# Two places for turned X, a new order of steps, and a shorter last dispatch in a banded attention with a soft mixture of experts

## The chip, the cores and the metric

The kernel runs on one core of one Trainium2 chip. The core has TensorE (PE, with its weight loads as PEld), VectorE (DVE), ScalarE (ACT), GpSimdE (POOL) and SyncE (SP, which issues most transfers), and 16 DMA engines. The metric is device time in microseconds (us); a kernel's time is the median of its runs. A profiled execution is one more run, with a record of each instruction.

## The reference

```python
def _attn_ref(q, k, v, n_global, n_local):          # B, H, S, D = 4, 8, 768, 64
    scores = scale * np.matmul(q, k.transpose(0, 1, 3, 2))
    rel = pos[:, None] - pos[None, :]
    is_global = pos[None, :] < int(n_global)         # 8
    is_local = (rel >= 0) & (rel < int(n_local))     # 96
    dist = np.where(is_global & ~is_local, float(n_local), np.abs(rel))
    scores = scores - slopes[:, None, None] * dist
    a = softmax(np.where(is_global | is_local, scores, -1e9))
    return np.matmul(a, v)

def _moe_ref(x, phi, w1, w2):                        # x: 3072 x 512, 8 experts, 4 slots each
    logits = x @ phi
    d = softmax(logits, over tokens); c = softmax(logits, over slots)
    slot_input = d.T @ x
    slot_out[e] = np.maximum(slot_input[e] @ w1[e], 0) @ w2[e]
    return c @ slot_out
```

Each query sees the first 8 keys and the 96 before it. The attention's output, 3072 tokens by 512, is the input X of the mixture: 32 slots are filled from all tokens, pass through two layers of weights (32 MB in all), and are spread over the tokens again.

## The kernel before

**Attention.** There are 16 units, u = 0 to 15: four batches by four pairs of heads. A unit is a row of steps. `load_qk` and `load_v` bring its inputs in, each into one of two places that alternate with u. `scores` (three steps, TensorE) multiplies queries and keys by bands of 120 into one of two pairs of PSUM banks (`sc`). `biased` (three steps, DVE) adds the table of the mask and the slope, and keeps the maximum. `max_t` and `max_r` (TensorE, DVE) make one shift of it. `exponential` (two heads, ACT) writes weights in float32, `w_hi` (ACT) casts them to float16, `w_lo` (three parts per head, POOL, or DVE as `w_lo_dve`) writes the rest that the cast left. `v_hi` and `v_lo` split v in the same way. `values` (per head, TensorE) multiplies 39 small products into the bank `x`. `ev_recs` and `ev_mul` (DVE) divide by the sums and write X. `tr` (two halves, TensorE) turns X and `tr_copy` (ACT, or DVE as `tr_copy_dve`) copies the turned half, 480 or 288 columns, into one of three places, the list `xtb`: a part of the tile `xta`, of `xtt` and of `tt`. `logits` (each second unit) multiplies the last two turned X with phi.

**Between batches** the steps `logits_half`, `logits_all`, `strip_exp`, `by_token`, `dispatch` and `dispatch_sum` carry the softmax over tokens on and add what the batch gives to the slots. For the last batch `last_dispatch` does this in one piece, with eight PSUM banks of which four are taken over from `sc` (the class `LeftBanks`, which hands banks out in a ring of six: the tags l0 to l3, and two of the pool `psm`).

**Mixture.** `hidden` (twice, four experts each) multiplies the slots with w1, `hidden_t` turns the result, `project` (twice two times) multiplies with w2 into 320 and then 192 output columns, `weights_by_slot` and `blocks_by_slot` bring the weights of the tokens into the tile `ct`, `combine` multiplies them with the slots' outputs and copies each product to an output buffer, which goes to memory.

**What sets the order.** `ORDER`, a list of steps written out in the file, holds the attention and the loads. It is walked once; each engine gets its instructions in that order and works them off one after the other. Transfers are issued by SP in the same order, and a transfer whose place is still being read holds up the ones behind it in SP's queue.

**Weights.** There are 32 pieces of 1 MB (128 x 2048). Ten have tiles of their own (`weights`). Others are loaded into tiles of the attention, when these come free: `piece` loads a whole one, `free(i)` loads into region i of the list `spaces`, `extra` loads the columns of a tile that the attention never uses. One piece lies in parts (`part`, the list `tails`): in a small tile `spare` and behind the ends of other tiles. A second piece has its first columns in `spare2` (`first`) and the rest where the first weight piece was, once that is used up.

**In the last dispatch** the function `warm_x` (L592 to L595) issues six matmuls whose product nobody reads. `warm` (L597 to L599) does the same at the start of the attention, 37 times.

Of the kernel before, what the change touches and what calls it, by code (L numbers as in the profile page):

```python
# [342 lines left out]
def tile_attention_moe(ctx: ExitStack, tc: tile.TileContext, qk, v, phi, w1, w2, nn, out):  # L343
# [34 lines left out]
    v16 = keep.tile([P, WP], F32, name="v16")  # L380
# [843 lines left out]
```

## Time and profile before

| | us |
|---|---|
| median of 3 runs | 195.08 |
| runs | 194.43 to 195.15 |
| the profiled execution | 194.77 |
| its span, first to last instruction | 193.0 |
| TensorE busy | 174.8 |
| DVE busy | 158.1 |
| ACT busy | 124.9 |
| POOL busy | 95.6 |

In the span the attention lasts to about 131 us, the last dispatch to 138, the two hidden layers and the first projection to 165, the second projection to 178. The last instruction that computes ends at 183, and the output's last transfers at about 190. 61.4 MB are moved in all. Rows of the profile name the source line, the engine, the operation and the tiles (out<-in); a row's first two numbers are start and length in us. Rows of the tables give a count and a mean. Names such as `m`, `sc`, `x`, `ld`, `cp` and `ctp` are PSUM banks; `tb` holds a unit's weights in float32, `ph` their two float16 parts.

### The profile page before, as it was taken

How to read it: one execution, taken by the hardware profiler on the slowest of the kernel's cores; microseconds unless marked ns; L12 is line 12 of the kernel's file. 1: busy time of each engine (PE TensorE's matmuls, PEld its weight loads, DVE VectorE, ACT ScalarE, POOL GpSimd, SP SyncE). 2: the span in 40 equal slices, each digit the busy share in tenths (PEclk: the TensorE clock that was granted, in tenths of full speed). 3: DMA queues.
4: the chain of work that ended last, by engine and by line, in shares of the span. 5: the costliest groups of instructions: out<-in, count | busy, mean ns of one | idle time of the engine just before them, and what ended most of it. 6: DMA issues, size and time to landing. Idle time of an engine off the chain costs nothing.

```text
span 193.0 us, 6494 instructions
## 1 busy us (share of the span) xinstructions
PE 174.8 (91%) x2676; PEld 130.3 (68%) x2676; DVE 158.1 (82%) x396; ACT 124.9 (65%) x162; POOL 95.6 (50%) x122
## 2 busy tenths in 40 slices
PE   8699999999999999998999999989999999799600
PEld 2355689788888879977878797875453366488500
DVE  3699799999998998999699999986797999772700
ACT  3107779998999998999899999924024161461500
POOL 7211936996688795797786897360001040000000
PEclk9999999999999999999999999999999999999965
DMA  2996756999499959999828679999999999479793
GB/s 71 401 394 195 269 186 202 358 396 364 162 404 346 410 186 364 423 410 378 310 87 317 270 256 360 409 420 420 400 401 416 421 418 419 164 257 356 259 324 123
DMA packets 19015, 61.40 MB, mean 318 GB/s; under 512 B 1824, under 2 KB 9632, under 8 KB 16416
## 3 DMA queue, kind: packets, MB, share of 16 engines
q1 hardware_dynamic: 17088, 59.55, 80.7%
q10 hardware_dynamic: 1888, 1.35, 2.1%
q8 instruction: 23, 0.38, 0.8%
q14 instruction: 16, 0.13, 0.2%
HBM read 54.59 MB, written 6.29 MB: 316 GB/s over the span
## 4 chain that ended last, share of the span: by engine, by line
PE 67%; DVE 10%; DMA 6%; ACT 6%; issue 3%; POOL 2%; ACTq 0%; DVEq 0%; POOLq 0%
PE sc L610 17%; PE x L670 14%; PE hp L127 8%; PE x L161 7%; DVE tb L619 4%; PE m L697 4%; DMA raw<-in_qk_dram 3%; PE cp L234 3%; DMA vt<-in_v_dram 3%; PE x L599 3%; PE m L798 2%; PE m L730 2%; POOL ph L645 2%; DVE v L588 2%; DVE xn L685 2%
## 5 line engine op out<-in xcount | busy, mean ns | idle before, releaser
L645 POOL TENSOR_TENSOR ph<-tb,ph 128x432 f16<-128x432 f32 x83 | 84.9, 1055 | 31.6 <-ACT ph L638 26.4
L635 ACT ACTIVATE tb<-tb,nb 128x1296 f32<-128x1296 f32 x32 | 43.1, 1373 | 9.9 <-DVE nb L631 9.9
L610 PE MATMUL sc<-raw 64*128 64x216 f32 (+2 forms) x448 | 45.7, 339 | 2.6 <-DMA raw<-in_qk_dram 1.6
L610 PEld LDWEIGHTS sc<-raw 64*128 64x128 f32 x448 | 37.0, 186 | 10.0 <-issue 4.0
L638 ACT CAST ph<-tb 128x1296 f16<-128x1296 f32 x31 | 39.4, 1269 | 4.9 <-PE x L670 4.3
L670 PE MATMUL x<-v,ph 128*128 128x65 f16 (+1 forms) x1209 | 41.7, 193 | 0.0
L670 PEld LDWEIGHTS <-ph 128*128 128x128 f16 x1248 | 39.8, 97 | 0.3
L588 DVE SCALAR_TENSOR_TENSOR v<-vt,v 128x896 f16<-128x896 f32 x16 | 18.7, 1171 | 0.5 <-ACT v L581 0.4
L619 DVE CUSTOM_DVE_ANT_1 tb<-sc,tt,mx 128x864 f32<-128x864 f32 x16 | 17.8, 1113 | 1.0 <-PE sc L610 0.3
L685 DVE CUSTOM_DVE_ANT_1 xn<-x,rcall 120x448 f32<-120x448 f32 x31 | 18.2, 619 | 0.4
L187 POOL TENSOR_TENSOR wp<-lnat,wp 120x512 f16<-120x512 f32 (+1 forms) x3 | 3.6, 1209 | 26.4 <-ACT wp L186 26.4
L581 ACT ACTIVATE v<-vt 128x896 f16<-128x896 f32 x14 | 13.3, 949 | 3.9 <-DMA vt<-in_v_dram 3.9
L697 PE MATMUL m<-ident,xn 120*128 120x120 f32 x105 | 15.4, 274 | 0.0
L197 DVE STREAM_TRANSPOSE wp<-wp 32x192 f32<-32x192 f32 (+1 forms) x32 | 12.9, 403 | 0.8
L697 PEld LDWEIGHTS m<-ident,xn 120*128 120x128 f32 x105 | 10.8, 141 | 1.6 <-issue 0.5
L127 PE MATMUL hp<-wp,sl 128*32 128x512 f32 x80 | 11.6, 595 | 0.0
L645 DVE TENSOR_TENSOR ph<-tb,ph 128x432 f16<-128x432 f32 x13 | 10.5, 815 | 0.1
L619 DVE CUSTOM_DVE_ANT_1 tb<-sc,xta,mx 128x864 f32<-128x864 f32 x8 | 8.9, 1108 | 1.3 <-PE sc L610 1.2
L619 DVE CUSTOM_DVE_ANT_1 tb<-sc,xtt,mx 128x864 f32<-128x864 f32 x8 | 8.9, 1113 | 0.4 <-PE sc L610 0.2
L619 DVE CUSTOM_DVE_ANT_1 tb<-sc,tt 128x864 f32<-128x864 f32 x8 | 8.4, 1054 | 0.9 <-POOL ph L645 0.4
L599 PE MATMUL x<-const-bfloat16-1.0 128*1 128x512 bf16 x37 | 9.2, 378 | 0.0
L234 PE MATMUL cp<-sots,ct 128*128 128x320 f32 (+1 forms) x48 | 8.4, 311 | 0.5 <-DVE sots L218 0.4
(224 smaller groups left out, 248.9 us busy)
## 6 DMA issues: line engine op xcount, KB each, us to landing
wp<-in_w_dram SPq DMA_DIRECT2D x15, 1024.0 KB, 8.9
raw<-in_qk_dram SPq DMA_DIRECT2D x15, 832.0 KB, 5.3
vt<-in_v_dram SPq DMA_DIRECT2D x16, 448.0 KB, 5.8
tb<-in_w_dram SPq DMA_DIRECT2D x3, 1024.0 KB, 7.4
raw<-in_w_dram SPq DMA_DIRECT2D x2, 1024.0 KB, 14.8
raw<-in_w_dram SPq DMA_DIRECT2D x2, 832.0 KB, 6.3
ph<-in_w_dram SPq DMA_DIRECT2D x2, 768.0 KB, 9.1
out_dram<-ph SPq DMA_DIRECT2D x2, 480.0 KB, 4.7
```

The costliest lines, as they stand in the source:

```text
L127: nc.tensor.matmul(out=hp[n][32 * s:32 * s + 32, :], lhsT=slv(a, c, s), rhs=w1(e, c // 2)[:, (c % 2) * DF + 512 * n:(c % 2) * DF + 512 * n ...
L234: nc.tensor.matmul(out=cp[:, w * i:w * i + w], lhsT=ct[:, t * P:t * P + P], rhs=sot, start=True, stop=True)
L588: nc.vector.scalar_tensor_tensor(out=vlo[k].rearrange("p j i d -> p (j i) d"), in0=vraw[k].rearrange("p j i d -> p (j i) d"), scalar=V_SC, ...
L599: nc.tensor.matmul(out=xx[0:1, 0], lhsT=busy_in[:, 0:1], rhs=busy_in, start=True, stop=True)
L610: nc.tensor.matmul(out=z[:, i, at:at + n], lhsT=r_[r, KCOL[j]:KCOL[j] + KR], rhs=r_[r, KW + KB * j:KW + KB * j + n], start=True, stop=True)
L619: nc.vector.tensor_tensor_reduce(out=tb(u)[:, :, BW * k:BW * k + BW], in0=sc[(3 * u + k) % 2][:, :, 0:BW], in1=table.unit(u % NP, k), scal ...
L635: nc.scalar.activation(out=t, in_=t, func=AF.Exp, bias=nbs[u], scale=T_SC)
L638: nc.scalar.copy(out=blocks(phi_[i])[:, :, 0:QW], in_=tb(u)[:, i].rearrange("p (s c) -> p s c", c=QW))
L645: (engine or nc.gpsimd).tensor_tensor(out=blocks(plo_[i])[:, c, 0:QW], in0=tb(u)[:, i].rearrange("p (s c) -> p s c", c=QW)[:, c], in1=bloc ...
L670: nc.tensor.matmul(out=x[:, (D + 1) * t:(D + 1) * t + d], lhsT=w[:, c:c + P], rhs=vv[:, j, i, 0:d], start=False, stop=(z == len(ops) - 1), ...
L685: nc.vector.tensor_tensor_reduce(out=xnb[(u // 2) % 3][:, :, c:c + D], in0=by_tile(x_bank(u, i))[0:KB, :, 0:D], in1=rcall[:, m, :].unsquee ...
L697: nc.tensor.transpose(out=m[:, at:at + KB], in_=xnb[(u // 2) % 3][:, t, P * (p % 2):P * (p % 2) + P], identity=ident[0:KB, 0:KB])
```

## The change

Five things are edited, and the list `ORDER` is another.

- `xtb` has two entries in place of three: the part of `tt` is gone, and `tt` shrinks from 2496 to 2048 columns. A turned X now goes to place u % 2. `spaces` has 17 regions in place of 18.
- `spare` holds 512 columns in place of 256 and `spare2` 448 in place of 256, so `part(0)` and `first` load more, and the piece in parts has four parts in place of five.
- For the last unit, `tr_copy` and `tr_copy_dve` halve each copy: the first half on ACT, the second on DVE.
- In `last_dispatch` the two calls of `warm_x` are gone, and each bank is named by its number in the ring (`at`).
- `by_slot(0)` stands ahead of the second half of the first projection and its copies are all on ACT; it stood behind that projection together with `by_slot(1)`.

```diff
-ORDER = [('load_v', 1), ('load_qk0', 0), ('load_phis', 0), ('load_qk', 0), ('load_v', 0),
+ORDER = [('load_v', 1), ('load_qk0', 0), ('load_phis', 0), ('load_qk', 0), ('load_v', 0),
...
-    tt = keep.tile([P, 2 * TABW + S], F32, name="tt")
+    tt = keep.tile([P, WP], F32, name="tt")
...
-    xtb = [xta[:, 0:S], xtt[:, 0:S], tt[:, 2 * TABW:2 * TABW + S]]
+    xtb = [xta[:, 0:S], xtt[:, 0:S]]
+    XTN = len(xtb)
...
-    spare = keep.tile([P, HF], F32, name="spare")
-    tails = [(0, HF, spare)] + [(HF * (2 * k + 1), HF * (2 * k + 3), tbt[i][:, WP:WP + 2 * HF]) for k, i in enumerate((1, 2, 0))]
-    tails.append((7 * HF, WP, tt[:, WP:WP + HF]))
+    spare = keep.tile([P, 2 * HF], F32, name="spare")
+    tails = [(0, 2 * HF, spare)] + [(2 * HF * k, 2 * HF * (k + 1), tbt[i][:, WP:WP + 2 * HF]) for k, i in ((1, 1), (2, 2), (3, 0))]
...
-    spare2 = keep.tile([P, 256], F32, name="spare2")
+    spare2 = keep.tile([P, 448], F32, name="spare2")
...
     def tr_copy(u, k):
         a, n = ((0, 4 * KB), (4 * KB, S - 4 * KB))[k]
-        nc.scalar.copy(out=xtb[u % 3][:, a:a + n], in_=ms.pop((u, k))[:, 0:n])
+        if u == last:
+            m = ms.pop((u, k))
+            nc.scalar.copy(out=xtb[u % XTN][:, a:a + n // 2], in_=m[:, 0:n // 2])
+            nc.vector.tensor_copy(out=xtb[u % XTN][:, a + n // 2:a + n], in_=m[:, n // 2:n])
+            return
+        nc.scalar.copy(out=xtb[u % XTN][:, a:a + n], in_=ms.pop((u, k))[:, 0:n])
...
-        mt = tile()
+        mt = tile(1)
         nc.tensor.transpose(out=mt[:, 0:P], in_=top.to_broadcast([P, P]), identity=ident)
-        warm()
-        warm()
...
-        mx = [tile(), tile()]
+        mx = [tile(2), tile(3)]
...
-        ml = tile()
+        ml = tile(4)
...
-        md, mz = [tile(), tile()], tile()
-        mg = tile()
+        md, mz = [tile(0), tile(1)], tile(2)
+        mg = tile(3)
...
     project(0, 0)
     moe.hidden_t(left, hss[1], hts[1])
+    for _, args in by_slot(0):
+        nc.scalar.copy(**args)
     moe.blocks_by_slot(spf[1], tps[1], (2, 0))
     nc.scalar.copy(out=ct[:, 3 * S:4 * S], in_=tps[1][:, 0:S])
     project(0, 1)
     slots_out(0)
-    copies = by_slot(0) + by_slot(1)
+    copies = by_slot(1)
     combine(0, 12, ((2, "DA", "S"),))
```

Counted over the list, POOL gets three `w_lo` more and DVE three fewer (nine leave DVE, six come to it); `v_hi` of unit 15 goes from ACT to DVE and `w_hi` of its first head from DVE to ACT; `v_hi` of unit 1 goes to POOL and those of units 0 and 7 to ACT. Six `tr_copy` change from ACT to DVE, and six others from DVE to ACT. SP has `load_qk` 1 to 4 and `load_v` 3 and 2 ahead of the first weight piece, and the `extra` loads, which were spread over the whole attention, now all come in its second half.

DVE at the start, behind the second `biased` of unit 0. L619 (now L613) is `biased`, its second row reads the maximum out; L339 writes the table of a pair of heads, L588 is `v_lo`, L631 (now L625) `max_r`. Before:

```order
L339 TENSOR_SCALAR tt<-tt 128x1728
L619 ISA tb_96,mx<-sc_177,tt,mx 128x2x432
L619 ISA mx 128x1
L619 ISA tb_97,mx<-sc_178,tt 128x2x432
L619 ISA mx 128x1
L631 ISA m,nb<-m,shift 128x128
L631 ISA nb 128x1
L339 TENSOR_SCALAR xta<-tt 128x1728
L588 SCALAR_TENSOR_TENSOR v_101<-vt,v_101 128x896
```

and with the change:

```order
L588 SCALAR_TENSOR_TENSOR v_101<-vt,v_101 128x896
L613 ISA tb_96,mx<-sc_177,tt,mx 128x2x432
L613 ISA mx 128x1
L339 TENSOR_SCALAR tt<-tt 128x1728
L625 ISA m,nb<-m,shift 128x128
L625 ISA nb 128x1
L588 SCALAR_TENSOR_TENSOR v_101<-vt,v_101 128x896
L613 ISA tb_97,mx<-sc_178,tt 128x2x432
L613 ISA mx 128x1
L339 TENSOR_SCALAR xtt<-tt 128x1728
```

Both `v_lo` come earlier, the first `max_r` stands ahead of the first `biased` of unit 1, and another table is written there.

TensorE in the last dispatch: `ld` are the banks of `LeftBanks`, `m` and `x` older banks, `dn` and `ex` the weights by token and by strip, `lsb` the logits. Before:

```order
L798 MATMUL m<-xn_106,dn 32x256 x7
L833 MATMUL ld<-ident,state 128x128
L595 LDWEIGHTS ident
L595 MATMUL x<-ident 128x256
...
L844 MATMUL ld<-ident,ex 120x128 x2
L775 MATMUL ld<-ident,lsb 120x128 x2
L798 MATMUL ld<-xn_107,dn 32x256 x7
```

and with the change:

```order
L799 MATMUL m<-xn_106,dn 32x256 x7
L834 MATMUL ld<-ident,state 128x128
L843 MATMUL ld<-ident,ex 120x128 x2
L776 MATMUL ld<-ident,lsb 120x128 x2
L799 MATMUL ld<-xn_107,dn 32x256 x7
```

The six matmuls of L595 are gone, and nothing else is moved.

ACT around the first combine: L148 copies the turned hidden layer, L994 (now L998) and L1004 (now L996 and L1005) write `ct`, L237 copies a product to an output buffer. Before:

```order
L148 COPY wp_92<-htp 128x512
L994 CAST ct<-wp_91 128x768
L237 COPY ph_99<-cp 128x320
L1004 CAST ct<-ctp 128x480 x2
L237 COPY ph_99<-cp 128x320
```

and with the change:

```order
L148 COPY wp_92<-htp 128x512
L996 CAST ct<-ctp 128x480
L996 CAST ct<-ctp 128x288
L998 CAST ct<-wp_91 128x768
L237 COPY tb_96<-cp 128x320
L1005 CAST ct<-ctp 128x480
L237 COPY tb_96<-cp 128x320
```

One of the two casts of 480 columns, and one of 288 that DVE had, now stand ahead of the projection's second half.

More of the change, by code (lines that the diff above doesn't have):

```diff
@@ L405, in tile_attention_moe @@
               ("ph0", (0, 2 * PH)), ("ph1", (0, 2 * PH)), ("v16", (0, VV)), ("v16", (VV, 2 * VV)),
-              ("vt", (0, VC)), ("vt", (VC, 2 * VC)), ("tt", (0, 2 * TABW)), ("tt", (2 * TABW, WP)), ("xta", (0, S)), ("xta", (S, S + TABW)),
+              ("vt", (0, VC)), ("vt", (VC, 2 * VC)), ("tt", (0, 2 * TABW)), ("xta", (0, S)), ("xta", (S, S + TABW)),
               ("xtt", (0, S)), ("xtt", (S, S + TABW)), ("xn", (0, XH))]
@@ L455, in first_of @@
     def first_of(k):
-        load_w([npl], 0, 256)
+        load_w([npl], 0, 448)
     def part_of(i):
@@ L565, in tile_attention_moe, with tile @@
         pool = None
-        def tile(self, shape, dtype, name, tag):
+        def tile(self, shape, dtype, name, tag, at=None):
             if self.pool is None:
@@ L570, in tile @@
                 self.pool = banks.enter_context(tc.tile_pool(name="psl", bufs=1, space=PSUM))
-            self.n += 1
+            self.n = self.n + 1 if at is None else at
             k = self.n % 6
@@ L589, in v_lo @@
                                        in1=vhi[k].rearrange("p j i d -> p (j i) d")[:, :, 0:D], op0=ALU.mult, op1=ALU.subtract)
-    idb = ident.bitcast(BF16)
-    def warm_x(u):
-        for n in (256, 256, P):
-            nc.tensor.matmul(out=xx[:, 0, 0:n], lhsT=idb[:, 0:P], rhs=idb[:, 0:n], start=True, stop=True)
     def warm(u, count):
@@ L701, in tr_copy @@
         a, n = ((0, 4 * KB), (4 * KB, S - 4 * KB))[k]
-        nc.scalar.copy(out=xtb[u % 3][:, a:a + n], in_=ms.pop((u, k))[:, 0:n])
+        if u == last:
[4 more added lines that the diff above has]
+        nc.scalar.copy(out=xtb[u % XTN][:, a:a + n], in_=ms.pop((u, k))[:, 0:n])
     def tr_copy_dve(u, k):
+        if u == last:
+            return tr_copy(u, k)
         a, n = ((0, 4 * KB), (4 * KB, S - 4 * KB))[k]
-        nc.vector.tensor_copy(out=xtb[u % 3][:, a:a + n], in_=ms.pop((u, k))[:, 0:n])
+        nc.vector.tensor_copy(out=xtb[u % XTN][:, a:a + n], in_=ms.pop((u, k))[:, 0:n])
     als, dns = {}, {}
@@ L729, in logits_of @@
             n = min(SW, S - SW * s)
-            nc.tensor.matmul(out=ms[u][32 * s:32 * s + 32, 0:n], lhsT=phis[:, units[u - k][1], :], rhs=xtb[(u - k) % 3][:, SW * s:SW * s + n],
+            nc.tensor.matmul(out=ms[u][32 * s:32 * s + 32, 0:n], lhsT=phis[:, units[u - k][1], :], rhs=xtb[(u - k) % XTN][:, SW * s:SW * s + n],
                              start=(k == 1), stop=(k == 0), skip_group_check=True)
@@ L817, in dispatch_sum, with last_dispatch, tile @@
             add_slots(b, m, slice(0, HF if b == B - 2 else DM))
-    def last_dispatch(left, warm):
+    def last_dispatch(left):
         b = B - 1
-        def tile():
-            return left.tile([P, 512], F32, name="ld", tag="x")
+        def tile(at):
+            return left.tile([P, 512], F32, name="ld", tag="x", at=at)
         mo = psm.tile([P, 512], F32, name="m", tag="m")
@@ L891, in table_pair @@
         table.pair(p)
-    steps = dict(piece=piece_of, free=free, part=part_of, first=first_of, extra=extra, load_qk0=load_qk0, load_phis=load_phis, keys=keys, warm_x=warm_x, warm=warm,
+    steps = dict(piece=piece_of, free=free, part=part_of, first=first_of, extra=extra, load_qk0=load_qk0, load_phis=load_phis, keys=keys, warm=warm,
                  table_a=table_a, table_b=table_b, table_pair=table_pair, load_qk=load_qk, load_v=load_v, v_hi=v_hi, v_hi_act=v_hi_act, v_hi_dve=v_hi_dve, v_lo=v_lo,
@@ L903, in tile_attention_moe @@
     left = LeftBanks()
-    rest = last_dispatch(left, lambda: warm_x(last))
+    rest = last_dispatch(left)
     fl = keep.tile([P, 12], F32, name="fl")
@@ L989, in combine, with by_slot @@
         moe.combine(left, ct, n, sots[:, at:at + w], obs, out, t0, plan)
+    def by_slot(b):
+        return moe.weights_by_slot(left, sps[b], ct, [(4 * (t % 2) + t // 2, TN[t], S * b + KB * t) for t in range(NJ)])
     project(0, 0)
     moe.hidden_t(left, hss[1], hts[1])
+    for _, args in by_slot(0):
+        nc.scalar.copy(**args)
     moe.blocks_by_slot(spf[1], tps[1], (2, 0))
@@ L996, in tile_attention_moe @@
     slots_out(0)
-    def by_slot(b):
-        return moe.weights_by_slot(left, sps[b], ct, [(4 * (t % 2) + t // 2, TN[t], S * b + KB * t) for t in range(NJ)])
-    copies = by_slot(0) + by_slot(1)
+    copies = by_slot(1)
     combine(0, 12, ((2, "DA", "S"),))
```

6 lines of the change are left out of this document (3 added, 3 removed).

## Prediction

> **What bounds the kernel now.** I read the page first, then busy time in stretches, then the waits of TensorE, then the timelines of DVE, POOL and PE at the places that the change touches. The page says that TensorE is the fullest engine and DVE the next:
>
> ```profile
> PE 174.8 (91%) x2676; PEld 130.3 (68%) x2676; DVE 158.1 (82%) x396; ACT 124.9 (65%) x162; POOL 95.6 (50%) x122
> ```
>
> The stretches (start and end in us, length, then busy time and instructions per engine, TensorE's granted clock, DMA share, GB/s) are the attention from the first values step, the last dispatch, the hidden layer with the first projection, the first combine, and the second projection, with the output's first writes:
>
> ```profile
> 24.00:36.30 12.30, 12.13 (x229) 10.65 (x228) 11.68 (x29) 10.86 (x11) 7.79 (x9) 1.00 0.66 240
> 36.30:50.00 13.70, 13.59 (x248) 11.49 (x249) 13.18 (x30) 12.68 (x15) 12.23 (x13) 1.00 0.84 322
> 50.00:70.00 20.00, 19.74 (x381) 17.15 (x382) 19.00 (x47) 19.49 (x24) 15.94 (x17) 1.00 0.85 321
> 70.00:90.00 20.00, 19.75 (x368) 17.39 (x362) 18.65 (x45) 18.97 (x23) 15.24 (x16) 1.00 0.98 388
> 90.00:110.00 20.00, 19.55 (x351) 15.99 (x351) 17.67 (x49) 18.61 (x22) 16.54 (x17) 1.00 0.72 264
> 110.00:131.00 21.00, 19.80 (x397) 16.56 (x395) 20.22 (x51) 16.79 (x25) 13.01 (x14) 1.00 0.89 348
> 131.00:138.40 7.40, 6.93 (x87) 4.21 (x89) 4.38 (x17) 1.90 (x8) 0.00 (x0) 1.00 1.02 414
> 138.40:165.40 27.00, 26.76 (x306) 13.62 (x303) 24.36 (x63) 7.88 (x13) 3.58 (x3) 1.00 1.02 411
> 165.40:172.00 6.60, 5.39 (x40) 3.89 (x44) 5.63 (x14) 4.63 (x13) 0.00 (x0) 1.00 0.42 150
> 172.00:178.40 6.40, 6.22 (x142) 5.32 (x141) 1.62 (x5) 0.99 (x4) 0.00 (x0) 1.00 0.99 347
> ```
>
> From 24 to 131 us PE is idle for 12.30 - 12.13, then 0.11, 0.26, 0.25, 0.45 and 1.20, in all 2.4 us of 107. Most of that stands in these waits of the same stretch:
>
> ```profile
> PE sc L610 <- DVE rcall L679: 0.7, 1, 0.7
> PE m L730 <- ACT xtt L702: 0.6, 1, 0.6
> ```
>
> So a new order of the same work has little to win between 36 and 131 us (about 2.3 us if every gap closes). What it can win lies in the start, where PE runs fillers until DVE and POOL have made the first weights, and in the three short stretches behind 131 us.
>
> A rule of the Trainium skill speaks against reading PE as full: Perfetto Trace Analysis, section Identifying the Most-Contended Engine, says that busy time of matmuls is no good measure and that the busy share of weight loads should be taken. By it the room would be 107 less the six weight-load figures, 89.2, or 17.8 us. The two longest waits above, 1.3 us together, don't bear that room out: nothing that the trace shows holds PE up for it.
>
> **Start.** DVE's rows where its order changes (start, length), then what POOL and PE make of it:
>
> ```profile
> 12.86 0.61 DVE L339 TENSOR_SCALAR tt<-tt 128x1728 bf16<-128x1728 bf16 x1
> 13.38 1.11 DVE L619 CUSTOM_DVE_ANT_1 tb<-sc,tt,mx 128x864 f32<-128x864 f32 x1
> 15.39 0.29 DVE L631 CUSTOM_DVE_ANT_0 m<-m,shift 128x128 f32<-128x128 f32 x1
> 16.12 1.08 DVE L588 SCALAR_TENSOR_TENSOR v<-vt,v 128x896 f16<-128x896 f32 x1
> 18.54 5.51 POOL L645 TENSOR_TENSOR ph<-tb,ph 128x432 f16<-128x432 f32 x5 [7.52 <-ACT ph L638]
> 24.29 0.18 PE L662 MATMUL x<-epsb,const-bfloat16-1.0 128*128 128x7 bf16 x1
> 27.10 2.95 POOL L645 TENSOR_TENSOR ph<-tb,ph 128x432 f16<-128x432 f32 x3 [3.04 <-ACT ph L638]
> 31.54 1.12 DVE L645 TENSOR_TENSOR ph<-tb,ph 128x432 f16<-128x432 f32 x1
> ```
>
> ```profile
> 21.88 1.74 PE sc L610 x20
> 26.88 1.06 DVE tb L619
> 35.67 0.54 DVE xn L685
> ...
> PE sc L610 <- DMA raw<-in_qk_dram: 1.6, 3, 0.8
> ```
>
> The last four are three pieces of the chain that ended last and one of PE's waits over the whole span. From 12.86 to the first max_r the new order on DVE is one v_lo (1.08), one bias step (1.11), one table (0.61): max_r at 15.66 against 15.39 now, so ACT and POOL begin 0.3 later. POOL's five low parts take 5.51 / 5 = 1.1 each; now the third one of head 0 is the fourth in the row (22.95), and PE takes two scores steps and a filler ahead of the first values (24.29). In the new order it is the third, at 18.54 + 0.3 + 3.3 = 22.1, and values stand ahead of these scores, so they start at about 22.3. Of these 2.0 us the two scores steps, done later, take back the 1.74 of the chain: 0.3 is left on PE. On DVE the low part at 31.54 (1.1) goes to POOL, which sat idle 3.04 us just before 27.10. From 26.88 to the end of the piece at 35.67 the chain runs nearly all on DVE, so this counts fully, unless POOL, with one part more, ends last. Bounds: a gain of 1.4 (both), and a loss of 0.8 if a load comes late, since load_v 3 now stands in SP's queue ahead of load_v 2 and load_qk 3 and waits for a v_lo (the longest wait of scores for qk is 0.8). I take -1.0, nearer to the gains, because PE needs load_qk 3 only after the first two values steps.
>
> **Steady attention.** DVE gives up three low parts net, 3.3 us at the 1.1 above, and POOL gets them; for unit 15 DVE and ACT exchange a cast each (v_hi against w_hi). None of it is PE's, and PE is full, so 0. Bounds: -2.3 (all gaps close) and +2.3 (as many new ones). Two places for turned X make each tr_copy wait for the logits of the pair before; the step list puts the logits ahead of it each time, so the cover is PE's other work; its price is a rival below.
>
> **Last unit and last dispatch.**
>
> ```profile
> 130.65 0.65 DVE L706 COPY tt<-m 128x480 f32<-128x480 f32 x1
> 131.46 0.66 DVE L706 COPY xta<-sc 128x480 f32<-128x480 f32 x1 [0.15 <-PE sc L697]
> 131.76 0.40 ACT L702 COPY xta<-x 128x288 f32<-128x288 f32 x1 [0.75 <-PE x L697]
> 133.55 0.49 ACT L760 ACTIVATE ex<-lsb,state 128x240 f32<-128x240 f32 x1 [1.39 <-DVE state L747]
> 133.81 0.71 PE L595 MATMUL x<-ident 128*128 128x256 bf16 x6
> 134.35 0.39 PE L844 MATMUL ld<-ident,ex 128*120 128x128 f32 x2
> 135.43 1.06 PE L798 MATMUL ld<-xn,dn 120*32 120x256 f32 x14 [0.47 <-ACT lnat L792]
> ```
>
> The copies now end at 132.1 on both engines. Halved, each engine would take about 0.4 and 0.3 from 131.4 (estimates, between half of 0.66 and 0.40 and the whole) and end there too, but the first 480 columns are ready 0.2 earlier: -0.15 (bounds -0.3, +0.1 for two more fixed costs). The filler at 133.81 goes; ex is ready at 134.04, so its transposes start 0.3 earlier. The first dispatch matmuls wait 0.47 us for lnat, which reads the bank that they get; in the new numbering they get another bank and wait only for dn on ACT. From 134.04 the transposes (0.3) and a copy of about the same length end near 134.7. So 134.8 in place of 135.43: -0.6 (bounds -0.3, the filler alone, and -0.7).
>
> **Combine.**
>
> ```profile
> 160.82 1.00 PE L161 MATMUL x<-xtt,wp 128*32 128x320 f32 x11 [0.24 <-ACT wp L148]
> 165.32 1.16 PE L208 MATMUL ctp<-idh,wp 120*128 120x120 f16 x14
> 167.61 1.03 ACT L1004 CAST ct<-ctp 128x480 fp32r<-128x480 f32 x2
> 168.22 0.19 PE L952 MATMUL ft<-ones,fl 128*1 128x1 f32 x2 [0.98 <-ACT ct L1004]
> ```
>
> Half of the 14 matmuls (0.58) moves ahead of 160.82, where PE idles 0.24: the projection ends 0.34 later. The flag's matmul no longer waits 0.98 for a bank, but the next output copies stand behind one ct copy on ACT and one on DVE, in place of two: 0.5 less on ACT (1.03 / 2), behind work that starts 0.34 later. Between that (-0.2) and the wait less the shift (-0.64) I take -0.3; bounds -0.7 and +0.3 (the shift alone).
>
> **Loads.** The heads loaded early (512 and 448 columns, now 256 each) leave less for the end, but extras go late: from raw0's release on I count 43648 columns in place of 41166, 1.27 MB, or 3.1 us at 411 GB/s. Cover: the last weights.
>
> ```profile
> 151.05 0.86 SPq L445 DMA_DIRECT2D raw<-in_w_dram  x2
> raw<-in_w_dram SPq DMA_DIRECT2D x2, 1024.0 KB, 14.8
> 175.27 0.35 PE L161 MATMUL x<-raw,wp 128*32 128x192 f32 x1
> ```
>
> They land near 151.05 + 14.8 = 165.9 and are used at 175.27: 9.4 us of cover. So 0; without it, up to 3.1 us. The stretch 165.4 to 172 has a DMA share of 0.42, so output that starts earlier finds room.
>
> **Sum.** -1.0 + 0 - 0.15 - 0.6 - 0.3 = -2.05 on the profiled execution (194.77, span 193.0), which lies 0.31 under the median of the three runs, 195.08: forecast 193.0. About 0.5% or 1.0 us is what can be told from no change.
>
> **Rivals.** (1) PE's fullness eats the start: what is early at 36 us waits later for ACT or DVE, and only the 1.05 behind 130 us stays: 194.0. For it: from 50 to 70 us DVE and ACT are busy 19.0 and 19.5 of 20 too. Against: DVE gets lighter. (2) Slower: the two places bite. ACT's tr_copy stands in ACT's queue ahead of exp and w_hi, and must wait for logits on PE. ACT waits for logits once now, in logits_half:
>
> ```profile
> ACT lsb L737 <- PE m L730: 1.2, 1, 1.2
> ```
>
> There are seven logits steps ahead of a copy; if three such waits reach PE through late w_hi, that is 3.6 - 2.05 = +1.5: 196.6. It decides from two such waits on. Against: ACT is late there at the end of the attention alone. (3) The room is larger than PE's busy time says: the skill's rule above, and the gaps of 2.4 us, of which 1.8 close: 191.2. (4) The change doesn't do what it says: order moves waits about without net effect, and the tail's gain ends in the drain of the output: 195.0. For it: DMA is at 0.99 from 172 us; against: it has 0.42 just before.
>
> **Numbers.** Forecast 0.46, (1) 0.19, (2) 0.15, (3) 0.12, (4) 0.08. All of the forecast's own range, 191.8 to 194.0, is faster by over 0.5%; with (3) and a third of (1) that makes 0.65 faster; two thirds of (1) and most of (4) make 0.18 within 0.5%; (2) and the rest 0.17 slower. All bounds at once would be -5.4 and +3.2; they hardly meet, so the range is 190.8 to 196.0.
>
> **What would show it.** Right: the first values start near 22.3, values of unit 2 about 1 us earlier than now; PE idle from 24 to 131 stays near 2.4 us; the last dispatch takes 0.6 less up to the hidden layer; no wait of ft. Wrong: new PE waits for scores on DVE or qk loads before 40 us; ACT xta or xtt waiting for PE L731 (logits) more than twice; PE waiting for DMA behind 138 us; an unchanged last out_dram.

## The result, and the profile after

The forecast was 193.0 us (190.8 to 196.0), faster. The changed kernel takes **197.50 us** in the median (196.92 to 197.62) against 195.12 (194.43 to 195.62) of the kernel before: a ratio of 1.0105 with an interval of 1.0065 to 1.0146. It is slower, and 1.5 us above the upper end of the range. Single executions of one kernel differ by about 1 us: among the experiments below, the profiled execution of the first lies 1.6 us above its kernel's median, that with the exchanged tables 1.1 below, and that with the earlier start 0.9 above.

The profiled execution takes 197.49 us with a span of 195.7, against 194.77 and 193.0: 2.7 us more, all inside the span. Its page, engines in the span:

```profile
PE 175.4 (90%) x2668; PEld 130.2 (67%) x2668; DVE 158.8 (81%) x393; ACT 126.8 (65%) x165; POOL 96.0 (49%) x124
```

TensorE is busy 0.6 us longer than before, so what is left of the 2.7 us is waiting. To find where, I cut both spans at the same `values` steps, the first head of unit 0, the second heads of units 2, 7 and 10, the first head of unit 12 and the second of unit 15, which is the last, and read busy time between these. The columns are start and end, length, busy time and instructions of PE, PEld, DVE, ACT and POOL, clock, DMA share, GB/s. Before:

```profile
6.50:24.29 17.79, 16.16 (x118) 9.40 (x118) 15.90 (x40) 8.13 (x7) 6.42 (x6) 1.00 0.82 306
24.29:39.83 15.54, 15.26 (x283) 13.32 (x283) 14.68 (x35) 14.00 (x14) 11.26 (x12) 1.00 0.73 264
39.83:74.56 34.73, 34.47 (x643) 29.84 (x641) 33.54 (x79) 32.62 (x40) 28.41 (x28) 1.00 0.85 320
74.56:96.51 21.95, 21.25 (x387) 18.49 (x384) 19.07 (x52) 20.66 (x24) 16.98 (x18) 1.00 0.98 383
96.51:107.42 10.91, 10.91 (x202) 9.04 (x200) 10.49 (x25) 10.47 (x12) 8.45 (x9) 1.00 0.64 230
107.42:128.44 21.02, 20.03 (x406) 16.40 (x405) 20.26 (x50) 18.98 (x27) 15.24 (x15) 1.00 0.85 332
```

After:

```profile
6.50:22.77 16.27, 15.15 (x102) 7.96 (x101) 14.50 (x36) 6.39 (x6) 4.44 (x5) 1.00 0.67 239
22.77:40.14 17.37, 16.32 (x298) 14.44 (x297) 16.87 (x36) 14.36 (x14) 13.49 (x14) 1.00 0.61 222
40.14:74.98 34.84, 34.72 (x640) 29.88 (x639) 32.62 (x80) 33.72 (x38) 29.13 (x29) 1.00 0.92 349
74.98:96.66 21.68, 21.68 (x394) 18.67 (x391) 20.53 (x50) 20.88 (x28) 16.83 (x18) 1.00 0.96 343
96.66:109.69 13.03, 11.46 (x204) 9.17 (x202) 10.79 (x29) 11.20 (x12) 11.28 (x12) 1.00 0.82 318
109.69:131.53 21.84, 19.73 (x406) 16.32 (x405) 20.68 (x48) 19.05 (x27) 12.31 (x13) 1.00 0.93 317
```

The first `values` step comes 1.52 us earlier (24.29 to 22.77). The five stretches behind it hold 103.91 us of TensorE's work in place of 101.92, so 1.99 us are only put off. Of these, 1.06 are made up for in the first of the five, by 40.14, and the other 0.93 behind it. They are the scores, grouped by line between the first and the last `values` step (busy time and mean ns, then idle time ahead), before and after:

```profile
L610 PE MATMUL sc<-raw 64*128 64x216 f32 (+2 forms) x364 | 37.0, 339 | 1.0 <-DVE rcall L679 0.7 <-DVE mx L619 0.3
```

```profile
L604 PE MATMUL sc<-raw 64*128 64x216 f32 (+1 forms) x384 | 39.0, 338 | 2.7 <-DMA raw<-in_qk_dram 1.6 <-DVE mx L613 1.1
```

Idle time in the five, length less busy time, goes from 0.28 to 1.05, from 0.26 to 0.12, from 0.70 to 0, from 0 to 1.57, and from 0.99 to 2.11: in all 2.62 more. So the last `values` step comes at 131.53 in place of 128.44: -1.52 + 1.99 + 2.62 = +3.09. From there to the end of the span it is 64.17 us in place of 64.56, or -0.39, and 3.09 - 0.39 = 2.70.

Three of the five lost, the first, the fourth and the last, and the waits of TensorE over the whole span name what held it up (waits in us: total, times, longest):

```profile
PE sc L604 <- DMA raw<-in_qk_dram: 2.7, 3, 1.6
PE m L776 <- DVE xtt L707: 1.3, 1, 1.3
...
PE sc L604 <- DVE mx L613: 1.1, 1, 1.1
```

The wait for `mx` (last row) lies right behind the first `values` step, that for q and k mostly in the stretch from 96.66, and that for `xtt` in the one from 109.69. Each of the three has a chain of its own.

**The start.** TensorE, DVE and POOL around the first `values` step, timelines of the changed kernel:

```profile
18.32 0.60 DVE L339 TENSOR_SCALAR xtt<-tt 128x1728 bf16<-128x1728 bf16 x1
19.27 5.23 POOL L639 TENSOR_TENSOR ph<-tb,ph 128x432 f16<-128x432 f32 x5 [11.82 <-ACT ph L632]
22.77 0.18 PE L656 MATMUL x<-epsb,const-bfloat16-1.0 128*128 128x7 bf16 x1
23.56 1.41 DVE L339 TENSOR_SCALAR xta<-tt 128x1728 bf16<-128x1728 bf16 x1
25.00 1.06 DVE L613 CUSTOM_DVE_ANT_1 tb<-sc,xta 128x864 f32<-128x864 f32 x1
26.13 1.08 PE L604 MATMUL sc<-raw 64*128 64x216 f32 x12 [1.05 <-DVE mx L613]
```

The table written into `xta` takes 1.41 us, and POOL's row of five lasts until 24.50. The same step into `xtt`, 5 us earlier and before POOL began, took 0.60. It stands ahead of the first `biased` of unit 2, and TensorE waits 1.05 us for that one's bank.

**The loads.** Three pieces of the chain that ended last (start, length), and what they release:

```profile
95.53 1.37 DVE v L588
96.92 0.33 SPq L471
97.34 8.30 DMA raw<-in_qk_dram
...
105.69 1.00 PE L604 MATMUL sc<-raw 64*128 64x216 f32 x8 [1.57 <-DMA raw<-in_qk_dram]
```

`load_qk` 14 stands in SP's queue behind a `load_v`, whose place a `v_lo` still reads; its data then take 8.3 us to land, and TensorE waits 1.57. From 84 to 104 us, before and after, the transfers are these (same columns as the stretches):

```profile
84.00:104.00 20.00, 19.30 (x362) 16.00 (x361) 17.68 (x45) 18.33 (x22) 15.44 (x16) 1.00 0.76 279
```

```profile
84.00:104.00 20.00, 20.00 (x381) 16.88 (x378) 18.78 (x49) 19.21 (x22) 16.19 (x17) 1.00 1.00 378
```

The weights that the new order loads here fill the transfer engines: a DMA share of 1.00 in place of 0.76.

**The end of the attention.** The chain from 123 to 126 us:

```profile
123.34 1.24 DVE ph L639
124.57 0.54 DVE v L584
125.11 0.37 DVE xtt L707
...
125.62 0.62 PE m L776 x4
```

`by_token` (L776) needs a bank that holds a turned X. DVE frees it with a copy (L707), which stands in DVE's queue behind a low part (L639) and the cast of unit 15's v (L584). In the last of the six stretches POOL is busy 12.31 us, where it was 15.24 before.

### The profile page after: what moved, and what is told of

The parts are those of the page before. It is cut to its first block, busy times and chain, and to the rows that moved or that the text cites. A ratio compares the mean times of both kernels' runs of the same rounds, so it can differ in the third digit from the quotient of the medians.

```text
span 195.7 us, 6491 instructions
## 1 busy us (share of the span) xinstructions
PE 175.4 (90%) x2668; PEld 130.2 (67%) x2668; DVE 158.8 (81%) x393; ACT 126.8 (65%) x165; POOL 96.0 (49%) x124
## 4 chain that ended last, share of the span: by engine, by line
PE 68%; ACT 8%; DMA 7%; DVE 7%; issue 2%; SPq 1%; ACTq 1%; DVEq 0%
PE sc L604 18%; PE x L664 13%; PE hp L127 8%; DMA raw<-in_qk_dram 7%; PE x L161 7%; PE m L691 4%; PE x L593 4%; PE m L731 3%; PE cp L234 3%; ACT ph L632 3%; ACT tb L629 2%; DVE tb L613 2%; PE m L620 1%; DVE ph L639 1%; PE ld L799 1%
## 5 line engine op out<-in xcount | busy, mean ns | idle before, releaser
L639 POOL TENSOR_TENSOR ph<-tb,ph 128x432 f16<-128x432 f32 x86 | 86.5, 1037 | 37.4 <-ACT ph L632 30.4
L629 ACT ACTIVATE tb<-tb,nb 128x1296 f32<-128x1296 f32 x32 | 43.6, 1375 | 6.4 <-DVE nb L625 6.3
L632 ACT CAST ph<-tb 128x1296 f16<-128x1296 f32 x32 | 40.7, 1271 | 5.6 <-PE x L664 3.1
L588 DVE SCALAR_TENSOR_TENSOR v<-vt,v 128x896 f16<-128x896 f32 x16 | 19.8, 1238 | 0.6 <-ACT v L581 0.4
L613 DVE CUSTOM_DVE_ANT_1 tb<-sc,tt,mx 128x864 f32<-128x864 f32 x16 | 17.7, 1104 | 2.0 <-PE sc L604 0.7
L613 DVE CUSTOM_DVE_ANT_1 tb<-sc,xta,mx 128x864 f32<-128x864 f32 x8 | 8.9, 1116 | 0.7
L613 DVE CUSTOM_DVE_ANT_1 tb<-sc,xtt,mx 128x864 f32<-128x864 f32 x8 | 8.9, 1115 | 0.6
L613 DVE CUSTOM_DVE_ANT_1 tb<-sc,tt 128x864 f32<-128x864 f32 x8 | 8.4, 1050 | 0.6 <-PE sc L604 0.4
L701 ACT COPY xta<-m 128x480 f32<-128x480 f32 (+1 forms) x13 | 6.2, 480 | 4.1 <-PE m L691 3.9
```

The lines of the kernel that those rows point to most:

```text
L588: nc.vector.scalar_tensor_tensor(out=vlo[k].rearrange("p j i d -> p (j i) d"), in0=vraw[k].rearrange("p j i d -> p (j i) d"), scalar=V_SC, ...
L613: nc.vector.tensor_tensor_reduce(out=tb(u)[:, :, BW * k:BW * k + BW], in0=sc[(3 * u + k) % 2][:, :, 0:BW], in1=table.unit(u % NP, k), scal ...
L629: nc.scalar.activation(out=t, in_=t, func=AF.Exp, bias=nbs[u], scale=T_SC)
L632: nc.scalar.copy(out=blocks(phi_[i])[:, :, 0:QW], in_=tb(u)[:, i].rearrange("p (s c) -> p s c", c=QW))
L639: (engine or nc.gpsimd).tensor_tensor(out=blocks(plo_[i])[:, c, 0:QW], in0=tb(u)[:, i].rearrange("p (s c) -> p s c", c=QW)[:, c], in1=bloc ...
```

## Experiments

Kernels are named by their edit. Ratios are to the kernel before on the same chip, with their interval. Diffs show steps of `ORDER` unless they show code.

### What the loads cost

```diff
 ('scores', 12, 2)
+('load_qk', 14)
...
-('load_qk', 14)
 ('biased', 13, 0)
```

> The changed kernel with one step moved: load_qk 14 stands directly behind scores(12,2), ahead of load_v 13, as soon as its buffer is free. Theory A (SP's queue): the load of pair 14 was issued at 97.34 us, behind load_v 13, which waits for v_lo(11) on DVE (ends 96.89), though scores(12,2) had left its buffer at 93.28; now it is issued near 93.4, lands by 101.7, and PE's wait of 1.57 us for it ahead of scores(14,0) is gone: 197.5 - 1.6 = 195.9 us, if nothing else has become the bound by then. Rival (the fullness of the other engines): POOL's low parts run without a gap from 104.34 to 110.17 us and set the pace there, so PE's wait turns into another wait behind it: 197.2 to 197.5, with no wait for qk in the profile.

196.35 us, ratio 1.0047 (1.002 to 1.0075). The load leaves SP's queue 3.4 us earlier, but the chain and TensorE show that the data come little sooner:

```profile
93.97 11.19 DMA raw<-in_qk_dram
...
105.21 1.00 PE L604 MATMUL sc<-raw 64*128 64x216 f32 x8 [0.44 <-DMA raw<-in_qk_dram]
```

11.2 us in place of 8.3: SP's queue was only a part of the cause, and with the transfer engines full, the weights ahead of it may be the other. So the next kernel puts these three loads behind it as well:

```diff
-('extra', 4)
 ('biased', 12, 0)
-('piece', 9)
...
-('extra', 8)
...
 ('load_qk', 14)
+('extra', 4)
+('piece', 9)
+('extra', 8)
```

> The changed kernel with load_qk 14 directly behind scores(12,2), as in the run before, and three weight loads (extra 4, piece 9, extra 8: 1.3 MB) moved behind it. Theory B (DMA engines): with load_qk 14 alone moved, its data took 11.2 us from issue to landing (93.97 to 105.2) where the median of these loads is 6.1, since the DMA engines' share was 0.98 to 1.02 from 84 to 100 us and the weights issued at 87.8 to 92.0 go first; with 1.3 MB less ahead it lands within 8 us, PE has no wait ahead of scores(14,0), and the time is 196.35 - 0.4 = 195.9 us. Rival (the order of the loads does not matter, the sum of the bytes does): the weights now delay load_v 13 and load_qk 15, a wait of the same 0.4 us or more shows for one of them: 196.3 to 196.8.

196.48 us, ratio 1.0053 (1.0027 to 1.0079). The load now takes 6.2 us from issue to landing, at a DMA share that is still 0.99 from 84 to 104 us, so the weights ahead of it were the other part. The wait is gone, and the last `values` step comes at 129.95 in place of 131.04 (0.58 of that lead is there at unit 4's second head already, up to which both have the same steps). But the time is that of the kernel before it, against what I had expected. Together the two edits take away about 0.6% (1.0105 to 1.005, with intervals that overlap), and all of that goes with the first. Nor is the 1.57 of the one profile a fixed price: in four other kernels below with these loads in the same order, the load takes 7.1 to 7.7 us, and TensorE waits for it 0.65, 0.59 and 0.46 us, and in one not at all.

### What the table costs

```diff
 ('scores', 1, 1)
-('table_pair', 3)
+('table_pair', 2)
...
-('table_pair', 2)
 ('biased', 2, 0)
+('table_pair', 3)
```

> The changed kernel with two table steps exchanged: table_pair 2 (needed by the bias of unit 2) is made at 18.3 us, where table_pair 3 (needed by unit 3) was, and table_pair 3 behind biased(2,0). Theory A (start): the 1.05 us that PE waits at 26.13 for scores(2,2) come from DVE, where table_pair 2 took 1.41 us beside POOL's low parts (0.60 where POOL was idle) right ahead of biased(2,0); biased(2,0) now starts near 23.7, the wait goes, and the second values step starts at 26.1 in place of 27.13: 197.5 - 1.0 = 196.5 us. Rival (what is early at the start is lost before 50 us, as the 1.5 us of the first values step were): the wait goes and the end stays at 197.3 to 197.6. Table_pair 3, now beside POOL, is expected to take about 1.4 us in place of 0.60 by both.

196.10 us, ratio 1.0023 (0.9998 to 1.0047): this one exchange takes back about three quarters of the loss. DVE, then the stretch that answers to 22.77 to 40.14:

```profile
18.38 0.60 DVE L339 TENSOR_SCALAR xta<-tt 128x1728 bf16<-128x1728 bf16 x1
23.63 1.05 DVE L613 CUSTOM_DVE_ANT_1 tb<-sc,xta 128x864 f32<-128x864 f32 x1
...
22.84:38.92 16.08, 16.08 (x297) 14.52 (x296) 15.76 (x36) 14.36 (x14) 13.50 (x14) 1.00 0.67 241
```

`biased` starts 1.4 us earlier, and TensorE has no idle time left there. The table that now comes second, at 24.60, takes 0.60 too, not the 1.4 that I had expected: POOL's row of five had just ended. Unit 2 begins its second head at 38.92, against 39.83 in the kernel before: **-0.91, and -1.0 was the prediction's term.** But the lead is lent. From there to the last `values` step TensorE is busy for 87.61 us, against 86.67 in the kernel before, with 302 matmuls of the scores in place of 294: the 0.94 us that were put off beyond unit 2 take it back. The wait of 1.57 for `load_qk` 14 isn't there either, though nothing was done to it: TensorE is 1.2 us earlier, and the load is issued 1.3 us earlier (96.01).

### What the last stretch costs

By moving `by_token` forward, ahead of the work that frees its bank late:

```diff
 ('tr', 13, 1)
+('by_token', 11)
+('tr_copy_dve', 13, 1)
 ('v_hi_dve', 15)
-('tr', 13, 0)
...
-('tr_copy_dve', 13, 1)
-('tr_copy_dve', 13, 0)
-('by_token', 11)
...
 ('values', 14, 1)
+('tr', 13, 0)
 ('w_lo_dve', 15, 0, 0)
+('tr_copy_dve', 13, 0)
```

> The changed kernel with three steps of the last stretch moved: by_token 11 stands ahead of tr(13,0) and so takes the bank of tr(12,1) in place of that of tr(13,1); the copy of tr(13,1) stands ahead of v_hi 15 on DVE; tr(13,0) and its copy come behind values(14,1). Theory A: the 1.27 us that PE waits at 125.62 come from the two turning banks (by_token waits for DVE's copy of tr(13,1), which stands behind a low part and the cast of V); by_token starts at about 123.9, values(14,1) at 124.7 in place of 126.08, and 0.6 to 1.3 us of it arrive at the end, the lower value where ACT's row of cast, exp and two copies (about 3.5 us behind 123.9) sets the last w_hi: 196.2 to 196.9 us. Rival: ACT and DVE, both full from 115 to 128 us, set that stretch, and the wait only shifts to logits(13) (now 0.49 us for xta): 197.3 to 197.6.

197.75 us, ratio 1.0117 (1.0078 to 1.0155): nothing is won. The 1.3 of L776 are gone, and others stand in their place:

```profile
PE m L691 <- ACT dn L789: 0.6, 1, 0.6
PE sc L604 <- DVE ph L639: 0.5, 1, 0.5
```

So taking this one wait away is worth nothing: the stretch is 21.78 us long in place of 21.84. The other way is to make DVE lighter there and POOL heavier, on top of the exchanged tables and with whole last copies:

```diff
-('w_lo_dve', 13, 0, 0)
+('w_lo', 13, 0, 0)
...
-('v_hi_dve', 15)
+('v_hi', 15)
...
-('w_lo_dve', 15, 0, 2)
+('w_lo', 15, 0, 2)
```

> The changed kernel with the two tables exchanged (196.1 us), the last copies whole as before, and three instructions of the last stretch given from DVE to POOL: w_lo(13,0,0), w_lo(15,0,2) and the cast of V of unit 15. Theory C (DVE and ACT together set the last stretch, while POOL is busy 12.3 of 21.8 us there, 15.2 of 21.0 in the kernel before): the stretch from values(12,0) to values(15,1), 21.85 us, falls to about 21.0; with 0.2 for the copies 196.1 - 0.85 - 0.2 = 195.1 us. Rival (POOL lengthens what DVE does beside it: 1.24 in place of 0.60 for a low part on DVE, 1.4 to 1.7 in place of 1.08 for v_lo): the stretch stays at 21.7 to 21.9, 195.9 us.

195.59 us, ratio 0.9994 (0.9959 to 1.0029). The stretch from unit 12's first `values` step to the last one:

```profile
107.65:128.89 21.24, 19.74 (x407) 16.33 (x405) 19.29 (x45) 19.05 (x27) 16.52 (x17) 1.00 0.93 316
```

21.24 in place of the 21.85 that it takes with the exchanged tables alone, DVE 1.4 us lighter (20.69 there) and POOL busy for 16.5 (13.8); in the kernel before it was 21.02. With both mends of the loads and the early `by_token` added:

> The changed kernel with all of these edits together: tables exchanged, load_qk 14 early with the three weight loads behind it, the last copies whole, three instructions of the last stretch on POOL, and by_token 11 ahead of tr(13,0) with the copy of tr(13,1) ahead of the cast of V. Theory: the losses are separate and add up: 196.1 (tables) - 0.2 (copies) - 0.3 (load) - 0.85 (last stretch) = 194.8 us, below the 195.6 of the kernel before. Rival (the last stretch takes back what comes early, as by_token ahead of tr did): 195.7 to 196.1 us.

197.42 us, ratio 1.011 (1.0063 to 1.0156). The stretch takes 23.1 us, with a wait of TensorE for `xmax` of 1.8 us. The sum of the parts that I had expected, 194.8, doesn't come. Without the early `by_token`, with one copy given from ACT to DVE as well:

```diff
-('tr_copy', 10, 0)
...
 ('ev_mul', 12, 1)
+('tr_copy_dve', 10, 0)
```

> The changed kernel with the edits that held in the runs so far and none that did not: tables exchanged, load_qk 14 early with three weight loads behind it, last copies whole, three instructions of the last stretch on POOL, by_token where the change has it; and one edit more: the copy of tr(10,0) goes from ACT to DVE, which waited 0.79 us at 112.8 while ACT's row has no gap over 0.5 us from 105.8 to 127. Theory E (the new order's loss is these separate waits and ACT's row): against the run with the tables, POOL and the copies (0.9994 of before) 0.4 us less for the load and 0.45 less for the copy: 0.995 of before, 194.6 to 194.9 us, level with before plus the tail alone (0.9972). Rival (the last stretch takes it back, as it did with by_token moved): 0.999 to 1.001 of before.

195.57 us, ratio 0.9982 (0.9954 to 1.001): so the early `by_token` had most likely spoiled what the other edits won, but the loads' mends and the copy bring nothing clear beyond 0.9994, and the last stretch is 21.63 us long. These edits bring the new order to the old one's time, and no further.

### The order or the two places?

The old memory (three places for turned X, 256 columns loaded early) with the new order, the new last dispatch and combine, and whole last copies; a few `free` steps have other numbers, since the regions count differently:

> The new step list with the memory of the kernel before: three places for turned X, heads of 256 columns each, the third place and its weights freed at the end; last dispatch, weights by slot as changed, last copies whole. Theory D (the order alone is the cause): the same losses as in the changed kernel, 1.05 us for scores(2,2), a wait ahead of scores(14,0), and 21.8 us from values(12,0) to values(15,1): 197.3 us (197.5 less 0.2 for the copies). Rival (the two places and the heads loaded early cost time by themselves, through waits of copies for logits or 0.9 MB more in flight at 84 to 104 us): 196.3 us or less, with one of these losses gone.

196.77 us, ratio 1.0079 (1.0047 to 1.011), 0.5 us less than I had expected. And the old order and memory, with the same new tail:

```diff
-        def tile(self, shape, dtype, name, tag):
+        def tile(self, shape, dtype, name, tag, at=None):
...
-            self.n += 1
+            self.n = self.n + 1 if at is None else at
...
-        warm()
-        warm()
...
+    for _, args in by_slot(0):
+        nc.scalar.copy(**args)
```

> The kernel before, with its step list, its three places and its loads, and only two parts of the change: the last dispatch with banks by number and without fillers, and the weights by slot of the first quarter ahead of the second projection (the last copies not halved). Theory A: these two parts keep what the traces of the two kernels show between the start of the second values step of unit 15 and the last output matmul: 0.56 us in the last dispatch (exp to first matmul 1.88 to 1.32), 0.23 us in the combine: 195.1 - 0.8 = 194.3 us. Rival: the end is held by the output's drain, which was 0.2 us longer in the changed kernel, and DVE or SP give the rest back: 194.9 to 195.2 us.

194.95 us, ratio 0.9972 (0.9948 to 0.9996). The two differ in the list of steps alone, its order and the engines that it names, and that is worth 1.0079 against 0.9972: 1.07%, or 2.1 us. The waits of the first are those of the changed kernel:

```profile
PE sc L610 <- DMA raw<-in_qk_dram: 2.4, 3, 1.1
PE m L775 <- DVE xtt L706: 1.3, 1, 1.3
...
PE sc L610 <- DVE mx L619: 1.1, 1, 1.1
```

So the new order is what costs, and the new tail gains. A price of the two places and the larger heads can't be told: 1.0105 and 1.0079 have intervals that overlap, and 0.2 us between them are the price of the halved copies, shown below.

### A start that is really earlier

On the old order with the new tail: the last filler ahead of the first `values` step goes, and POOL makes head 0's last low part one place earlier.

```diff
-('w_lo', 0, 1, 0)
+('w_lo', 0, 0, 0)
 ('max_r', 1)
...
-('w_lo', 0, 0, 0)
-('warm', 12, 3)
+('w_lo', 0, 1, 0)
```

> The kernel before with the changed tail (0.9972 of before) and one edit at the start: the filler ahead of the first values step (0.74 us) is gone, and w_lo(0,0,0) changes places with w_lo(0,1,0) on POOL, so that the first values step has its weights near 21.9 and starts behind the two scores steps at about 23.6 in place of 24.37, with no score moved behind it. My prediction's step (an earlier first values step is worth what PE's row gains): 0.7 us less at values(2,1) and at the end, 194.2 us. Rival (DVE's row from 26.9 to 35.7, which the chain of the kernel before runs along, sets the start): values(0,0) early, values(2,1) as before (39.8 to 39.9) with new waits of PE ahead of it, 194.9 us.

**194.36 us, ratio 0.9939 (0.9915 to 0.9963)**: faster than both kernels. TensorE:

```profile
23.52 0.18 PE L662 MATMUL x<-epsb,const-bfloat16-1.0 128*128 128x7 bf16 x1
25.27 0.32 PE L626 MATMUL m<-ident,mx 128*128 128x128 f32 x1 [0.38 <-DVE mx L619]
```

The first `values` step comes 0.85 earlier than with the new tail alone (24.37). What takes part of it back is visible too: 0.38 of waiting for DVE, and unit 2 begins its second head 0.30 earlier (39.62 against 39.92). No other work of TensorE was put behind the step. About half of the 0.6% is the new tail's (0.9972 alone), and since the two intervals overlap, the rest is likely the start's, but not beyond doubt. Next, DVE is relieved of one low part right behind it, to close that wait:

```diff
 ('values', 0, 0)
-('w_lo_dve', 0, 1, 1)
+('w_lo', 0, 1, 1)
```

> The kernel before with the changed tail and the earlier first values step (0.9939 of before), and one low part of the start, w_lo(0,1,1), given from DVE to POOL, which sits idle 2.36 us at 24.0. Theory F (DVE's row is what the early values step runs into: PE waits 0.6 us for DVE's nb ahead of values(0,1), 27.19 against a possible 26.6): DVE gets there 0.6 us earlier, the wait goes, values(2,1) starts at about 39.1 in place of 39.62, and the end is 0.3 to 0.5 us earlier: 0.9915 of before, 193.9 us. Rival (ACT's row of exp and cast sets values(1,*), as in the changed kernel, where the low parts given to POOL brought nothing): values(2,1) stays at 39.5 to 39.7, 0.994 of before, 194.4 us.

195.49 us, ratio 1.0006 (0.9977 to 1.0036): the gain is gone, against what I had expected. The wait for `mx` stays at 0.4, a new one of 0.4 for `xmax` comes at 30.99, and unit 2 begins its second head at 39.86, 0.24 later than without the edit. At the first heads of units 3 and 4 the lag is 0.47 (44.00 against 43.53) and 0.86 (51.91 against 51.05), with a wait for q and k ahead of unit 4 that is hardly longer (0.68 against 0.59), and at the last `values` step it is 0.96. Then, beside it, the cast of unit 15's v goes from ACT to POOL:

```diff
-('v_hi_act', 15)
...
 ('w_lo', 14, 1, 0)
+('v_hi', 15)
```

> The same with one instruction of the last stretch moved: the cast of V of unit 15 goes from ACT (0.96 us at 119.6, in a row without a gap from 117.5 to 127) to POOL, behind its low parts of unit 14, where it has 3.35 us idle. Theory C (ACT and DVE set the last stretch): values(12,0) to values(15,1) fall from 21.0 to 20.3 to 20.6, another 0.4 to 0.7 us: 0.989 of before, 193.4 us. Rival (POOL beside DVE lengthens v_lo and the low parts on DVE, and PE's 0.6 us for xtt stays): 20.9 to 21.1, no difference to the run without it.

197.85 us, ratio 1.0114 (1.0064 to 1.0164). Up to unit 14 the steps are those of the kernel just above, but here the wait for q and k ahead of unit 4 is 0.19, and the lag is gone behind it (51.04 and, at unit 12, 107.62, against 107.73 with the earlier start alone). The stretch of units 12 to 15 grows to 23.3 us, in which DVE is busy for 22.5 (20.3 in the kernel before). DVE and POOL at its end:

```profile
122.67 1.29 POOL L578 TENSOR_SCALAR v<-vt 128x896 f16<-128x896 f32 x1
123.08 1.56 DVE L641 CAST ph<-tb 128x1296 f16<-128x1296 f32 x1
126.08 0.95 DVE L770 SCALAR_TENSOR_TENSOR state<-state,al 128x1 f32<-128x1 f32 x1
```

The same rows of the kernel before, where ACT made that cast, read

```profile
122.88 0.82 DVE L641 CAST ph<-tb 128x1296 f16<-128x1296 f32 x1
125.15 0.21 DVE L770 SCALAR_TENSOR_TENSOR state<-state,al 128x1 f32<-128x1 f32 x1
```

What shortened the new order's last stretch, work for POOL, hurts the old one: DVE's steps on the path take 0.7 us more each beside it, and what follows them comes late. Which order stands it could be told only by running both.

## Why the prediction was wrong, and where it was right

**The start, -1.0: right up to the first `values` step, and wrong behind it.** That step came at 22.77, near the 22.3 that was forecast, and the scores put off weigh 1.99 where I had 1.74. What failed is "this counts fully": +0.31 at 39.83 against 40.14, with 0.93 us of the work put off still to do there, so +1.24 in all. Two things were wrong. I priced DVE's rows with 0.61 for a table and 1.08 for `v_lo`, from rows during which POOL stood still. Beside POOL the table ahead of unit 2's first `biased` takes 1.41, and TensorE waits the 1.05 us; a new wait for scores on DVE before 40 us was the sign named for it. The exchange takes this row out of the way and turns +0.31 into -0.91. It moves the whole row, though; the mis-size is 0.81 of it, by which I estimate -0.5 had the row stayed there and cost 0.60. And I took the scores for paid back within the start. They are paid back until the end of the attention: even with the tables exchanged the -0.91 meets 0.94 us of work put off, and nothing is left.

**Steady attention, "PE is full, so 0": wrong, by +1.85.** From unit 2's second head to the last `values` step it is 91.39 us in place of 88.61, 2.78 more, of which 0.93 is the work that the start owed. The rest is idle time, which changed by -0.14 - 0.70 + 1.57 + 1.12. This sum lies inside the bounds of ±2.3, but the reason given for the value taken, 0, was none. A full engine says that an order can win little; it doesn't say that it can't lose. The term had four stretches in it, and I read neither where the new order puts the loads among one another nor who frees the banks behind 120 us.

**Loads, 0: priced at the wrong place.** I asked whether the last weights come in time, and they did: TensorE waits for no transfer behind 138 us. But some of the columns that go late, and a whole piece that now goes early (issued at 90.58 in place of 104.17), are issued between 86 and 92 us. They fill the transfer engines where `load_qk` 14 needs them. The cover of 9.4 us belonged to another transfer. The count of columns doesn't come out either: by the step list 42752 are loaded from raw0's release on, not 43648, so 1586 more than before, 0.81 MB. It entered no term.

**The last unit's copies, -0.15: +0.19.** This is the time from the last `values` step to the second row of `ex`, which reads its sum out: 5.51 us before, 5.70 after, and 5.69 or 5.70 in each kernel with halved copies against 5.49 to 5.52 in each with whole ones (only the last experiment takes longer, 6.45). The halves don't run side by side, as the sum assumed. ACT and DVE:

```profile
134.54 0.36 ACT L698 COPY xtt<-sc 128x240 f32<-128x240 f32 x1 [0.24 <-PE sc L691]
134.85 0.28 ACT L698 COPY xtt<-x 128x144 f32<-128x144 f32 x1
134.93 0.41 DVE L699 COPY xtt<-sc 128x240 f32<-128x240 f32 x1 [1.11 <-ACT xtt L698]
```

DVE stands idle for 1.11 us ahead of its half of the bank `sc`. The last 0.39 of it, from 134.54, is ACT's half, and DVE starts when that has ended. Whole copies of two banks did overlap before (131.46 + 0.66 on DVE, 131.76 + 0.40 on ACT). The Trainium skill, PSUM — Partial Sum Buffer, section PSUM bank collisions raise a hardware error, says that two engines must not touch one bank in the same 32 partitions at once, reads against reads included and whatever the columns, and that the compiler puts a dependency between them; the trace agrees, with DVE's half 0.03 us behind the end of ACT's.

**The last dispatch, -0.6: right.** From the start of `ex` to its first matmuls it was 133.55 to 135.43, 1.88 us, and is now 1.32:

```profile
136.83 0.49 ACT L761 ACTIVATE ex<-lsb,state 128x240 f32<-128x240 f32 x1 [1.70 <-DVE state L748]
138.15 1.06 PE L799 MATMUL ld<-xn,dn 120*32 120x256 f32 x14
```

**Combine, -0.3: right, and given back.** From the hidden layer to the end of the last product it is 43.45 before and 43.21 after, -0.24, with no wait of `ft`. In its place TensorE's waits ahead of the products (`cp`, for `sots`, `ct` and an output buffer) grow from 0.4 to 1.8 us. And the output's drain behind it takes 11.42 in place of 11.20, and the sum had no term for the drain. So the 2.70 us are +1.24 at the start, +1.85, +0.19 and -0.56 (1.32 less 1.88), then -0.24 and +0.22. Without the halved copies the tail is worth more: -0.68 in the profiled execution of the old order with the new tail, and 0.28% in its ratio.

**The rivals.** The time was beyond all of them. Rival (2), two places that bite, with its 196.6 comes nearest, but its mechanism is absent: ACT waits for logits once, as before, and the new order is slow with three places too. Rival (1) saw that the start's lead would be lost, but by less: it had no loss beyond it. Missing was a rival in which the new order adds waits of its own at several places. And (3), a larger room, was not borne out: the best kernel here gains 0.6%, or 1.2 us, and half of that in the tail.

**What stays open.** The last stretch is told only in part. Relieving DVE of three steps takes away 0.6 of the 0.8 us that it is longer in one kernel and 0.2 in another with the same three steps, which gives DVE one copy more, and moving the wait alone takes nothing away; which step of the new order makes it late there, I didn't find. Nor why giving one low part at 25 us to POOL costs 0.7% in the runs: the lag of 0.96 in its profile isn't there in the next kernel, which has the same steps up to unit 14.

## What to carry to other kernels

Take the price of an operation from a row whose neighbour engines do what they will do in the new place: DVE's table cost 0.60 beside an idle POOL and 1.41 beside a working one, and moving it out of the way brought unit 2 forward by 1.2 us. An early first step that is bought by putting work behind it isn't yet a gain: count what the full engine still owes at the place where the lead is read. And a full engine is no cover: compare idle time between the same pieces of work, and look for what each queue, SP's too, now holds ahead of what the full engine needs. Halve a copy between two engines by banks, not by columns of one.
